# Gated mix of linear attention and a ReGLU layer: block products for down in seven first-half pairs, and one written order in the last projections

## The chip, the cores and the metric

The kernel runs on one core of one Trainium2 chip. The metric is the device time of one execution in microseconds (us). Before the change it is 1589.73 us, the median of three runs (1588.61 to 1591.07).

The core has five engines, each with its own queue of instructions that run in order: PE (TensorE, matrix products), DVE (VectorE), ACT (ScalarE), POOL (GpSimd) and SP (SyncE, which here only issues transfers). They wait for each other through semaphores.

## The reference

```python
def _A_ref(x, wqkv, w_phi, wo):          # linear attention, 32 heads of 18
    q, k, v = ...                         # x @ wqkv
    phi_q, phi_k = ...                    # softmax(+-(q or k) @ w_phi), joined
    kv, z = phi_k^T @ v, sum of phi_k
    return (phi_q @ kv) / (phi_q @ z + 1e-6) @ wo

def _B_ref(x, W_gate, W_up, W_down):
    gate = x @ W_gate
    up = x @ W_up
    gate = gate * (gate > 0)
    return (gate * up) @ W_down

g = _sigmoid((x * gate_w).sum(-1, keepdims=True))
return g * _A_ref(x, ...) + (1 - g) * _B_ref(x, ...)
```

All is float32, x has 2048 rows of 576, W_gate and W_up are 576 x 4608, W_down is 4608 x 576.

## The kernel before

Every float32 operand is split into a high part (rounded, made by ACT) and a low part (the rest, made by DVE), and a product is high x high + high x low + low x high on PE. Three stages follow each other.

**Attention (0 to about 340 us).** Keys, queries and values of 16 blocks of 128 rows, then for each of four blocks of 512 rows the sums, their inversion, `divide` (a matmul that spreads the inverse over the rows, a multiplication on DVE, then high part on ACT and low part on DVE) and `project_out`, which multiplies by the output weights and stores the rows to `att` in DRAM. `project_out(2, m)` and `project_out(3, m)` are the last ten. Between them the operands of the gated part are prepared: the weights of chunks 0 and 1 (`blocks`, `sums_of_blocks`, `block_sums`), and the seven operands of x (`operand_ahead` for three, `in_place` for four). PE, SP and POOL run that stage in program order (`in_order`). ACT and DVE are ordered by a scheduler there, with `behind` and `after` as limits.

**Gated part.** 4608 hidden columns are 36 chunks of 128, and a chunk for one half of the rows (1024) is a unit: units 0 to 35 for the first half, 36 to 71 for the second. Gate and up of a unit are formed together by seven products (a Strassen-Winograd scheme, `product`), one in each of seven steps j = 0 to 6, in the order 1, 5, 6, 2, 7, 3, 4. Each is 7 matmuls of 128x512. Products 1, 6, 7 and 4 gather in the PSUM tile `cx`, 5 and 3 in `ca`, 2 in `cy`. Partial sums are read from there on the way: g1 is a copy of `cx` after product 1 to which `cy` is added in step 4, u2 a copy of `ca` to which `cx` is added in step 5, g2 a copy of `cx` to which `ca` is added in step 6. Product 4 (step 6) may change `cx` only once u2 has read it.

Two chunks are a pair g. Its hidden tiles are ready after units 2g and 2g + 1, and the product with W_down (down) of pair q = g - 1 runs in the steps of units 2g (even) and 2g + 1 (odd), behind the product of each step. The addition of its result to the accumulators `ac` (DVE) follows one step later. In the second half pairs go by seven block products again (`down`: 14 products of 3 matmuls in two rows of blocks m = 0 and 1, and four of 2 matmuls for the last 64 columns). In the first half all pairs go plainly (`down_plain`: 8 outputs of 6 matmuls, two of 4). Block products need sums of down blocks (`down_sums_of_blocks`, POOL), differences of hidden tiles (`minus`, DVE), seven hidden tiles in high and low part in place of four, and 14 additions in place of 8. `plain_down` or `prepare_down` splits the raw down weights, `load_down` fetches the next.

In the first half the weights of the next chunk are also prepared in every unit: high parts on ACT, low parts `low_w` and, on 32 rows, `low_w_rows` on DVE, four sums of blocks on DVE. From unit 4 on a unit may end with one piece of `second_half`, which scales x for the second half (DVE). All five queues of the gated part are in program order, the order in which `step(u, j)` is written.

**End.** The last pair goes plainly, and the results are stored.

Of the kernel before, what the change touches and what calls it, by code (L numbers as in the profile page):

```python
# [15 lines left out]
P = 128  # L16
# [67 lines left out]
def gated_mix_kernel(  # L84
# [533 lines left out]
    def divide(b, k):  # L618

        R = RW[b]  # L620
# [4 lines left out]
        oh, ol = OW[b]  # L625
# [4 lines left out]
        nc.tensor.matmul(ps, spread[:, k], RD[b % 2], start=True, stop=True)  # L630
        r = R[:n, k]
        tt(out=r, in0=ps[:n], in1=r, op=MULT)
        nc.scalar.activation(oh[:n, k], r, AF.Copy)
        tt(out=ol[:, k] if k < 4 else oh[64:, k], in0=r, in1=oh[:n, k].bitcast(F32), op=SUB)
# [234 lines left out]
    def low_w_rows(o, a):  # L869
        tt(out=o[64:96, :, 2], in0=a[64:96, :, 2], in1=o[64:96, :, 2].bitcast(F32), op=SUB)  # L870
# [43 lines left out]
    def first_weights():  # L914
        with behind():
            blocks(0, high_w)
            low_parts(blocks, 0)
            sums_of_blocks(0)
        yield
        with behind():  # L920
            blocks(1, high_w)
            low_parts(blocks, 1)
        yield
        with behind():
            block_sums(0, high_w)
            sums_of_blocks(1)
        with behind():
            block_sums(1, high_w)
            low_parts(block_sums, 0)
        yield  # L930
        in_place(3)
        with behind():
            low_parts(block_sums, 1)
        yield
        for i in range(4, 7):
            in_place(i)
            yield

# [20 lines left out]
    def in_place(i):  # L959
        with behind():  # L960
            high_in_place(0, i)
            low_in_place(0, i)
            low_rest(0, i, tt)

    with in_order(tc, nc, nc.tensor, nc.sync, nc.gpsimd):
# [25 lines left out]
        for m in range(5):  # L991
# [11 lines left out]
            if m == 2:  # L1003
                with after(tc, nc, nc.vector, last_of(nc, nc.vector)):
                    invert(3)
                gather(3, 3, 2, 1, 0)
                whole(split_inverse(3))
                whole(x0)
        for m in range(5):
            project_out(2, m)  # L1010
            if m == 0:
                divide(3, 4)
                divide(3, 3)
                whole(x1)
            if m == 1:
                weights = first_weights()
                for k in (2, 1, 0):
                    divide(3, k)
                RS.close()
                pad = ctx.enter_context(tc.tile_pool(name="pad2", bufs=1, **R_))  # L1020
                pad.tile([P, 24], F32, name="pad2")
                xo2 = ctx.enter_context(tc.tile_pool(name="xo2", bufs=4, **R_))
                wop = ctx.enter_context(tc.tile_pool(name="wop", bufs=2, **R_))
                wraw = ctx.enter_context(tc.tile_pool(name="wraw", bufs=2, **R_))
                load_w(0)
                load_in_place(0, 3)
                load_rests(0, (3, 4, 5))
                load_w(1)
                for i in range(4, 7):
                    load_in_place(0, i)  # L1030
                whole(x2)
                load_rests(0, (6,))
                load_down(0)
                next(weights)
            if m > 1:
                next(weights)
        load_w(2)
        for m in range(5):
            project_out(3, m)
            if m < 3:  # L1040
                next(weights)
# [54 lines left out]
    def rest_weights(g, step):  # L1096
# [4 lines left out]
        elif step == 1:  # L1101
            tt(out=W4[g][:, 0:2, 1], in0=a, in1=W4[g][:, 0:2, 0].bitcast(F32), op=SUB)
            pt(out=a[:, 0], in0=a[:, 0], in1=a[:, 1], op=ADD)
# [38 lines left out]

    PLAIN = {1: (0, 0, 1), 2: (0, 1, 1), 3: (2, 0, 1), 4: (0, 0, 0), 5: (0, 1, 0), 6: (2, 0, 0),
# [35 lines left out]

    def down(g, s, bank):  # L1180
# [14 lines left out]
        if m == 0 and n in (1, 5, 2, 4):  # L1195
            w, r = {1: (0, 0), 5: (2, 1), 2: (1, 0), 4: (3, 1)}[n]
            if first and n in (1, 5):
                REST[r] = pm.tile([P, TB], F32, name=f"pm{r}")
            w = W4[g][:, w].rearrange("p s q -> p (s q)")
            mm(REST[r], w, h, first and n in (1, 5), False)  # L1200
            mm(REST[r], w, l, False, last and n in (2, 4))

        def add():
            i, t = ADDS[n]
            a = ACC[1, i, m, t]
# [116 lines left out]
    def step(u, j):  # L1322
# [4 lines left out]
        plain, was_plain = g < NG or g == 2 * NG - 1, q < NG  # L1327
# [3 lines left out]
        make = 0 < u < NC - 1  # L1331
        cx, ca, cy = (BANKS.get(n) for n in ("cx", "ca", "cy"))
# [20 lines left out]
        elif odd:  # L1353
            if j == 1:
# [28 lines left out]
        if make:  # L1383
# [4 lines left out]
            elif j == 1:  # L1388
                blocks(v, low_w)
                blocks(v, low_w_rows)  # L1390
# [4 lines left out]
            elif j == 4:  # L1395
                block_sums(v, low_w)
                block_sums(v, low_w_rows)
# [38 lines left out]
        if old and j == 5:  # L1436
            load_down(g)
# [30 lines left out]
        if j == 6 and u < NC:  # L1468
            if u >= 4:
# [163 lines left out]
```

## Time and profile before

| | |
|---|---|
| median of three runs | 1589.73 us |
| profiled execution | 1589.56 us |
| its span, first to last instruction | 1587.8 us |
| mean granted PE clock | 0.997 |
| POOL additions and subtractions on raw down weights (L1080 to L1083) | 136, all in the second half |

The page lists for each engine the time in which it was busy and its share of the span. The table of stretches gives the same for pieces of the span. A timeline row gives start, duration, engine, line, operation, output and inputs, the count of merged instructions, and in brackets the idle time before it with what ended it. Matmuls overlap: each lasts 0.39 us, but the next starts long before it ends, so the cost of one is read from starts or counts. A wait is the idle time that another engine or a transfer ended.

### The profile page before, as it was taken

The numbers are of one execution on the slowest core, as the hardware profiler recorded it, in microseconds if no ns is written. First come the engines' busy times: TensorE is split into PE (matmuls) and PEld (weight loads), VectorE is DVE, ScalarE is ACT, GpSimd is POOL, SyncE is SP. The second block draws the span as 40 slices with busy tenths as digits, with TensorE's granted clock in tenths as the row PEclk, the third lists the DMA queues.
The fourth block names the chain that finished last, engine by engine and source line by source line (L and its number), as shares of the span: only waits on it lengthen the run. The fifth ranks groups of instructions, "written<-read, shape, count | busy, mean of one in ns | idle before, by whom it ended". The sixth has DMA issues, their size and how long they took to land.

```text
span 1587.8 us, 20181 instructions
## 1 busy us (share of the span) xinstructions
PE 1570.8 (99%) x7823; PEld 1313.4 (83%) x7823; DVE 1190.8 (75%) x1865; ACT 559.0 (35%) x918; POOL 175.2 (11%) x243
## 2 busy tenths in 40 slices
PE   9999999999999999999999999999999999999998
PEld 9999995677888888888888888888888888888887
DVE  4997774577778777787777777777777777777777
ACT  4344335554333333333333334232233232222321
POOL 0126521110000000000000002111111111111110
PEclk9999999999999999999999999999999999999999
DMA  5365315587655576555554516543343343443432
GB/s 171 108 207 192 143 55 157 170 332 261 217 219 211 209 262 223 215 191 221 193 196 183 210 71 233 189 177 143 143 180 143 146 175 131 167 168 131 180 140 75
DMA packets 64539, 283.38 MB, mean 178 GB/s; under 512 B 6802, under 2 KB 17298, under 8 KB 55740
## 3 DMA queue, kind: packets, MB, share of 16 engines
q1 hardware_dynamic: 61228, 270.34, 47.0%
q0 software_dynamic: 2352, 10.11, 2.0%
q10 hardware_dynamic: 864, 1.65, 0.3%
q8 instruction: 61, 1.00, 0.3%
q14 instruction: 34, 0.28, 0.0%
HBM read 172.07 MB, written 108.60 MB: 177 GB/s over the span
## 4 chain that ended last, share of the span: by engine, by line
PE 95%; DVE 3%; ACT 1%; DMA 0%; issue 0%; POOL 0%; SPq 0%; ACTq 0%; POOLq 0%
PE cx L1128 29%; PE ca L1128 14%; PE pd L1168 12%; PE pd L1191 10%; PE cy L1128 7%; PE kv L175 4%; PE pk L175 3%; PE pq L175 3%; PE pm L1168 2%; PE pm L1191 2%; PE kv L421 1%; PE po L562 1%; PE pv L237 1%; PE pw L175 1%; PE ptr L379 1%; PE psf L259 1%
## 5 line engine op out<-in xcount | busy, mean ns | idle before, releaser
L1233 ACT ACTIVATE hh<-g 128x512 fp32r<-128x512 f32 x195 | 120.0, 624 | 458.5 <-DVE g L1290 289.2
L1206 DVE TENSOR_TENSOR ac<-pd,ac 128x512 f32<-128x512 f32 x238 | 164.1, 689 | 144.0 <-PE pd L1191 143.9
L1128 PE MATMUL cx<-xo,ws 128*128 128x512 f32 x1008 | 253.5, 391 | 3.3 <-ACT g L1294 3.3
L1128 PE MATMUL ca<-xo,ws 128*128 128x512 f32 x1008 | 251.9, 389 | 0.0
L1128 PE MATMUL cx<-xo,wb 128*128 128x512 f32 x1008 | 249.0, 389 | 1.5 <-DVE u L1415 1.5
L1128 PEld LDWEIGHTS cx<-xo,ws 128*128 128x128 f32 x1008 | 190.2, 189 | 43.3 <-ACT g L1294 3.7
L1128 PEld LDWEIGHTS cx<-xo,wb 128*128 128x128 f32 x1008 | 188.2, 188 | 42.5 <-DVE u L1415 1.9
L1128 PEld LDWEIGHTS ca<-xo,ws 128*128 128x128 f32 x1008 | 189.2, 188 | 39.3
L1168 PE MATMUL pd<-hh,wd 128*128 128x512 f32 x576 | 200.7, 389 | 0.0
L1191 PE MATMUL pd<-hh,wd 128*128 128x512 f32 x476 | 185.2, 389 | 0.0
L1174 DVE TENSOR_TENSOR ac<-pd,ac 128x512 f32<-128x512 f32 x144 | 99.1, 688 | 105.8 <-PE pd L1168 103.3
L1238 DVE TENSOR_TENSOR hl<-g,hh 128x512 fp32r<-128x512 f32 x195 | 135.7, 696 | 1.9 <-ACT hh L1233 0.2
L1294 ACT ACTIVATE g<-cx 128x512 f32<-128x512 f32 x144 | 85.0, 590 | 130.8 <-PE cx L1128 130.7
L1128 PE MATMUL cy<-xo,wb 128*128 128x512 f32 x504 | 127.3, 392 | 0.0
L1168 PEld LDWEIGHTS pd<-hh,wd 128*128 128x128 f32 x576 | 108.1, 188 | 22.6
L1091 ACT ACTIVATE wd<-wdr 128x384 fp32r<-128x384 f32 (+1 forms) x106 | 62.3, 606 | 143.4 <-DMA wdr<-wd 143.4
L1128 PEld LDWEIGHTS cy<-xo,wb 128*128 128x128 f32 x504 | 95.6, 190 | 20.0
L1168 PE MATMUL pd<-hl,wd 128*128 128x512 f32 x288 | 112.0, 389 | 0.0
L1191 PEld LDWEIGHTS pd<-hh,wd 128*128 128x128 f32 x476 | 89.3, 188 | 18.6
L1191 PE MATMUL pd<-hl,wd 128*128 128x512 f32 x238 | 92.6, 389 | 0.0
L831 POOL TENSOR_TENSOR xo<-xr,xo 32x512 fp32r<-32x512 f32 x5 | 8.3, 1669 | 615.9 <-ACT xo L847 615.9
L864 ACT ACTIVATE ws<-wr 128x1536 fp32r<-128x1536 f32 x36 | 53.7, 1491 | 46.6 <-DVE wr L888 46.6
(256 smaller groups left out, 2574.1 us busy)
## 6 DMA issues: line engine op xcount, KB each, us to landing
wsd<-ws SPq DMA_DIRECT2D x34, 1280.0 KB
ws<-wsd SPq DMA_DIRECT2D x34, 1280.0 KB
wbd<-wb SPq DMA_DIRECT2D x34, 960.0 KB
wb<-wbd SPq DMA_DIRECT2D x34, 960.0 KB
wr<-wgu SPq DMA_DIRECT2D x36, 768.0 KB
wdr<-wd SPq DMA_DIRECT2D x36, 576.0 KB
eT<-et SPq DMA_DIRECT2D x10, 594.0 KB
xt<-xb SPq DMA_DIRECT2D x7, 768.0 KB
```

The costliest lines, as they stand in the source:

```text
L175: nc.tensor.matmul(ps, w, m, start=i == 0, stop=i == len(pairs) - 1)
L237: nc.tensor.matmul(pv[i][c], m, w_[:, k, cs], start=k == 0 and n == 0, stop=k == 4 and n == 1)
L864: nc.scalar.activation(o[:, :, 0:3], a, AF.Copy)
L1091: nc.scalar.activation(o[:, 0], a, AF.Copy)
L1128: nc.tensor.matmul(ps, w, v, start=first and m == 0, stop=m == len(pairs) - 1, skip_group_check=True)
L1168: nc.tensor.matmul(ps, w, v, start=k == 0 and (i < 2 or first), stop=k == len(mms) - 1 and (i < 2 or last), skip_group_check=True)
L1174: tt(out=a, in0=ps, in1=a, op=ADD)
L1191: mm = lambda ps, w, v, a, z: nc.tensor.matmul(ps, w, v, start=a, stop=z, skip_group_check=True)
L1206: tt(out=a, in0=ps, in1=a, op=ADD)
L1233: nc.scalar.activation(h, src, AF.Copy)
L1238: tt(out=l, in0=src, in1=h.bitcast(F32), op=SUB)
L1294: nc.scalar.activation(a, ps, AF.Copy)
```

## The change

Two things are changed together.

Seven first-half pairs, g = 3, 5, 7, 9, 11, 13 and 15, take down by block products (`BY_BLOCKS`). The other first-half pairs stay plain. Their last 64 columns keep the plain weights, with one further hidden tile, key 8 (`REST_OF`), and so need no sums of those weights. In the odd unit of such a pair and in both units of the next one, the two operations of `low_w_rows` are run by POOL. The unit after such a pair has no piece of `second_half`. The raw down weights of a block pair that follows a plain one are fetched at step 1, not 5.

In the attention stage `divide` is cut in two (`quotient`, `operand_rows`). From the last block's divisions of k = 2, 1 and 0 on, ACT and DVE are in program order too, and the preparation of weights and operands is written out between the last projections.

```diff
+    def quotient(b, k):
...
         nc.tensor.matmul(ps, spread[:, k], RD[b % 2], start=True, stop=True)
         r = R[:n, k]
         tt(out=r, in0=ps[:n], in1=r, op=MULT)
+
+    def operand_rows(b, k):
...
         nc.scalar.activation(oh[:n, k], r, AF.Copy)
         tt(out=ol[:, k] if k < 4 else oh[64:, k], in0=r, in1=oh[:n, k].bitcast(F32), op=SUB)
...
+    def low_w_rows_aside(o, a):
+        low_w_rows(o, a, pt)
...
+        project_out(2, 0)
+        divide(3, 4)
+        divide(3, 3)
+        whole(x0)
+    with in_order(tc, nc, nc.tensor, nc.vector, nc.scalar, nc.gpsimd, nc.sync):
+        project_out(2, 1)
+        for k in (2, 1, 0):
+            quotient(3, k)
+        for k in (2, 1, 0):
+            operand_rows(3, k)
+        whole(x1)
...
+        project_out(3, 0)
+        block_sums(0, high_w)
+        low_parts(blocks, 1)
+        operand_low(0, 2)
+        load_rests(0, (6,))
         load_w(2)
+        low_parts(block_sums, 0)
+        high_in_place(0, 3)
+        project_out(3, 1)
+        low_of_place(3)
+        sums_of_blocks(1)
+        high_in_place(0, 4)
+        project_out(3, 2)
+        block_sums(1, high_w)
+        low_of_place(4)
+        high_in_place(0, 5)
+        project_out(3, 3)
+        low_parts(block_sums, 1)
+        low_of_place(5)
+        in_place(6)
+        project_out(3, 4)
...
+    BY_BLOCKS = range(3, NG - 2, 2)
+
+    def is_plain(g):
+        return g < NG and g not in BY_BLOCKS or g == 2 * NG - 1
...
+    REST_OF = ({1: (0, 0, 1), 5: (0, 1, 8), 3: (1, 1, 3), 2: (1, 0, 2)},
+               {1: (0, 0, 1), 5: (2, 1, 5), 2: (1, 0, 2), 4: (3, 1, 4)})
...
-        plain, was_plain = g < NG or g == 2 * NG - 1, q < NG
+        plain, was_plain = is_plain(g), is_plain(q)
...
+        rows_ = low_w_rows_aside if g in BY_BLOCKS and odd or q in BY_BLOCKS else low_w_rows
...
+            if g < NG and j < 2:
+                (high_h, low_h)[j]((g, 8), e2)
...
-                blocks(v, low_w_rows)
+                blocks(v, rows_)
...
-                block_sums(v, low_w_rows)
+                block_sums(v, rows_)
...
-        if old and j == 5:
+        if old and j == (1 if was_plain and not plain else 5):
             load_down(g)
...
-            if u >= 4:
+            if u >= 4 and not (old and q in BY_BLOCKS):
                 next(later_half, None)
```

The order of DVE around the start of unit 8, the even unit in which down of pair 3 begins. `ac` are additions into the accumulators, `hl` low parts of hidden tiles, `wb` and `ws` low parts of weights, `wr` sums of blocks, `g` and `u` the partial sums. Before, from the last addition of unit 7 to step 1 of unit 8:

```order
L1174 TENSOR_TENSOR ac<-pd_4622,ac 128x512
L1418 TENSOR_TENSOR g_4589<-ca,g_4589 128x512
L1290 SCALAR_TENSOR_TENSOR g_4589<-g_4589,u_4568 128x512
L335 TENSOR_TENSOR xb<-xb,ac 128x768
L1290 SCALAR_TENSOR_TENSOR g_4545<-g_4545,cx 128x512
L1238 TENSOR_TENSOR hl<-g_4589,hh 128x512
L867 TENSOR_TENSOR wb<-wr,wb 128x3x256
L870 TENSOR_TENSOR wb<-wr,wb 32x3x128
```

The same stretch of DVE with the change:

```order
L1190 TENSOR_TENSOR ac<-pd_4633,ac 128x512
L1442 TENSOR_TENSOR g_4596<-ca,g_4596 128x512
L1311 SCALAR_TENSOR_TENSOR g_4596<-g_4596,u_4572 128x512
L1308 TENSOR_TENSOR g_4414<-g_4596,g_4414 128x512
L335 TENSOR_TENSOR xb<-xb,ac 128x768
L1311 SCALAR_TENSOR_TENSOR g_4548<-g_4548,cx 128x512
L1308 TENSOR_TENSOR g_4457<-g_4596,g_4457 128x512
L1227 TENSOR_TENSOR ac<-pd_4671,ac 128x512
L1259 TENSOR_TENSOR hl<-g_4414,hh 128x512
L877 TENSOR_TENSOR wb<-wr,wb 128x3x256
L1102 TENSOR_TENSOR wd<-wdr,wd 128x384
```

Two differences (L1308), one addition and one pass over down weights come in, and the operation on 32 rows of `wb` goes to POOL.

Further on in unit 8 DVE had, before, from step 2 to u2 in step 5 (the three sums L885 to L887 ahead of it left out):

```order
L888 TENSOR_TENSOR wr<-wr 128x384
L1174 TENSOR_TENSOR ac<-pd_4695,ac 128x512
L867 TENSOR_TENSOR ws<-wr,ws 128x4x256
L870 TENSOR_TENSOR ws<-wr,ws 32x4x128
L1413 TENSOR_TENSOR g_4670<-cy,g_4670 128x512
L1174 TENSOR_TENSOR ac<-pd_4729,ac 128x512
L1415 TENSOR_TENSOR u_4693<-cx,u_4693 128x512
```

With the change DVE has there:

```order
L901 TENSOR_TENSOR wr<-wr 128x384
L1227 TENSOR_TENSOR ac<-pd_4671,ac 128x512
L1308 TENSOR_TENSOR g_4414<-g_4548,g_4414 128x512
L1259 TENSOR_TENSOR hl<-g_4457,hh 128x512
L1227 TENSOR_TENSOR ac<-pd_4695,ac 128x512
L1259 TENSOR_TENSOR hl<-g_4548,hh 128x512
L877 TENSOR_TENSOR ws<-wr,ws 128x4x256
L1437 TENSOR_TENSOR g_4692<-cy,g_4692 128x512
L1227 TENSOR_TENSOR ac<-pd_4671,ac 128x512
L1259 TENSOR_TENSOR hl<-g_4414,hh 128x512
L1439 TENSOR_TENSOR u_4721<-cx,u_4721 128x512
```

Three low parts, one difference and one addition more stand ahead of u2 (L1415, now L1439), and the row operation of `ws` is gone to POOL, where one of `wb`, the four sums of down blocks and one of `ws` now follow each other in each such unit.

The order of ACT at the end of the attention stage. `xo` are the high parts of x operands that are made in place, two rows for each; `o` are rows of a projection; the `g` at the end is the first copy of `cx`. Before:

```order
L864 ACTIVATE ws<-wr 128x4x384
L786 ACTIVATE o<-kv_3612 128x512
L864 ACTIVATE ws<-wr 128x4x384
L846 ACTIVATE xo<-xo 128x1024
L847 ACTIVATE xo<-xr 128x512
L846 ACTIVATE xo<-xo 128x1024
...
L847 ACTIVATE xo<-xr 128x512
L786 ACTIVATE o<-kv_3634 128x512
L788 ACTIVATE o<-kv_3652 64x512
L1294 ACTIVATE g_3716<-cx 128x512
```

With the change ACT has:

```order
L856 ACTIVATE xo<-xo 128x1024
L857 ACTIVATE xo<-xr 128x512
L796 ACTIVATE o<-kv_3602 128x512
L874 ACTIVATE ws<-wr 128x4x384
L856 ACTIVATE xo<-xo 128x1024
L857 ACTIVATE xo<-xr 128x512
L796 ACTIVATE o<-kv_3626 128x512
L856 ACTIVATE xo<-xo 128x1024
L857 ACTIVATE xo<-xr 128x512
L798 ACTIVATE o<-kv_3652 64x512
L1315 ACTIVATE g_3716<-cx 128x512
```

Of the four pairs of `xo` that stood between the weights `ws` of chunk 1 and the first copy of `cx`, two now stand ahead of those weights.

More of the change, by code (lines that the diff above doesn't have):

```diff
@@ L632, in divide @@
         tt(out=r, in0=ps[:n], in1=r, op=MULT)
+    def operand_rows(b, k):
+        n = P if k < 4 else 64
+        oh, ol = OW[b]
+        r = RW[b][:n, k]
         nc.scalar.activation(oh[:n, k], r, AF.Copy)
@@ L912, in low_parts @@
         f(u, low_w_rows)
[L914 to L937, printed above, removed]
     BEHIND = {}
@@ L959, in in_place, with low_of_place @@
     def in_place(i):
[L960 to L963, printed above, removed]
+        high_in_place(0, i)
+        low_of_place(i)
+    def low_of_place(i):
+        low_in_place(0, i)
+        low_rest(0, i, tt)
     with in_order(tc, nc, nc.tensor, nc.sync, nc.gpsimd):
@@ L1007, in gated_mix_kernel @@
                 whole(split_inverse(3))
[L1008 to L1036, printed above, removed]
```

44 lines of the change are left out of this document (33 added, 11 removed).

## The prediction

> **What bounds the kernel now.** I read the page first: the busy times, then the chain of work that ended last.
>
> ```profile
> PE 1570.8 (99%) x7823; PEld 1313.4 (83%) x7823; DVE 1190.8 (75%) x1865; ACT 559.0 (35%) x918; POOL 175.2 (11%) x243
> ...
> PE 95%; DVE 3%; ACT 1%; DMA 0%; issue 0%; POOL 0%; SPq 0%; ACTq 0%; POOLq 0%
> ```
>
> PE (TensorE) is nearly always busy and carries 95% of the chain. A matmul removed is therefore worth its own time, as long as nothing else becomes late, and any new wait of PE is lost in full. The table of 50 us stretches gives the price of a matmul and the room of the other engines. Its columns are length, then busy time and instructions of PE, weight loads, DVE, ACT and POOL, then PE's granted clock, DMA share and GB/s.
>
> ```profile
> 600.00:650.00 50.00, 50.00 (x222) 41.39 (x222) 40.16 (x61) 16.88 (x24) 0.00 (x0) 1.00 0.50 193
> 1050.00:1100.00 50.00, 50.00 (x222) 41.25 (x221) 35.84 (x60) 14.30 (x30) 6.44 (x14) 1.00 0.41 156
> ```
>
> In the first half of the gated part (600 to 650) PE does 222 matmuls in 50 us, one per 0.225 us. DVE (VectorE) is busy 40.2 of 50 us there, POOL (GpSimd) not at all. In the second half (1050 to 1100), where down already goes by block products and no gate and up weights are prepared, DVE has 35.8 of 50 us. So the first half, which is to get more DVE work, has the least room for it.
>
> PE's waits, the same for all times (total, times, longest), name the only other place with something to win, the stage around 300 to 372 us:
>
> ```profile
> PE cx L1128 <- ACT g L1294: 3.3, 1, 3.3
> PE cx L1128 <- DVE u L1415: 1.5, 1, 1.5
> PE kv L630 <- DVE R L632: 1.2, 2, 0.9
> ```
>
> **The matmuls removed.** A pair of chunks with plain down takes 8 outputs of 6 matmuls and 2 of 4, so 56; by block products 14 of 3 and 4 of 2, so 50. Seven pairs save 42 matmuls, 42 x 0.225 = **9.45 us**, if PE stays fed.
>
> **The DVE work added.** Each block pair adds on DVE 4 low parts of hidden tiles, 4 differences, 6 additions into the accumulators and four smaller passes over down weights in place of one long one. Six operations on 32 rows go from DVE to POOL. What matters is where this stands, since DVE now runs every operation in a written order. The timeline of DVE in a plain unit of before shows the distance from start to start (columns start, duration, instruction, idle before it):
>
> ```profile
> 603.42 0.69 DVE L1174 TENSOR_TENSOR ac<-pd,ac 128x512 f32<-128x512 f32 x1 [1.51 <-PE pd L1168]
> 604.02 0.68 DVE L1238 TENSOR_TENSOR hl<-g,hh 128x512 fp32r<-128x512 f32 x1
> 604.62 0.55 DVE L885 TENSOR_TENSOR wr<-wr 128x384 f32<-128x384 f32 x1
> 605.21 0.56 DVE L886 TENSOR_TENSOR wr<-wr 128x384 f32<-128x384 f32 x1
> ...
> 606.40 0.56 DVE L888 TENSOR_TENSOR wr<-wr 128x384 f32<-128x384 f32 x1
> 606.87 0.68 DVE L1174 TENSOR_TENSOR ac<-pd,ac 128x512 f32<-128x512 f32 x1
> 607.47 1.42 DVE L1094 TENSOR_TENSOR wd<-wdr,wd 128x1024 fp32r<-128x1024 f32 x2
> 608.81 1.22 DVE L867 TENSOR_TENSOR ws<-wr,ws 128x1024 fp32r<-128x1024 f32 x1
> ...
> 613.84 0.69 DVE L1174 TENSOR_TENSOR ac<-pd,ac 128x512 f32<-128x512 f32 x1 [1.20 <-PE pd L1168]
> 614.45 0.68 DVE L1418 TENSOR_TENSOR g<-ca,g 128x512 f32<-128x512 f32 x1
> 615.16 0.69 DVE L1290 SCALAR_TENSOR_TENSOR g<-g,u 128x512 f32<-128x512 f32 x1
> 615.77 0.95 DVE L335 TENSOR_TENSOR xb<-xb,ac 128x768 f32<-128x768 f32 x1
> 616.64 0.68 DVE L1290 SCALAR_TENSOR_TENSOR g<-g,cx 128x512 f32<-128x512 f32 x1
> ```
>
> An operation of 128x512 costs 0.60 us of DVE, 0.71 if the next one needs its result; four sums of blocks cost 3 x 0.59 + 0.47 = 2.24; an operation of 0.95 costs 0.87, and by the same 0.085 us of overlap one of 1.22 costs 1.14 and one of 0.55 costs 0.47.
>
> I count the worst unit, the even one after a block pair (unit 8, as the order of DVE in the part on the change shows it). Time 0 is where PE starts the unit. DVE was last idle for the addition in the step before: before, that stood 613.84 against a unit start of 613.64 + 7 x 0.225 = 615.21 by the row of PE,
>
> ```profile
> 613.64 3.34 PE L1128 MATMUL cx<-xo,wb 128*128 128x512 f32 x14
> ```
>
> so DVE starts at -1.37. From there to u2 = cx + ca stand: the step before, 0.60 + 0.71 + 0.71 + 0.60 (addition, g2, gate, difference); step 0, 0.87 + 0.60 + 0.60; step 1, 0.60 + 0.60 + 0.87 + 0.47; step 2, 0.60 + 0.60 + 2.24; step 3, 3 x 0.60; step 4, 0.60 + 0.60 + 1.14 + 0.60; step 5, 0.60 + 0.60 + 0.69. Together 17.30, so u2 is done at 15.93. PE wants it for product 4 after 42 product matmuls and 26 of down, 68 x 0.225 = 15.30. PE is stopped 0.63, and about 0.04 for the signal (before, 613.84 came that long after the matmul): **0.67 us**, with POOL costing nothing.
>
> In the odd unit after it (9) DVE catches up at step 2, 20 matmuls in (4.50, plus 0.20 until the last has drained and signalled: 4.70). Until u2 stand four additions, g1 and one low part (6 x 0.60), the sums (2.24), the low parts of the plain down weights (1.34, as 607.47 to 608.81) and of the sums' weights (1.14), and u2 itself (0.69): 9.01, done at 13.71. PE wants u2 after 60 matmuls, 13.50. Stop with the signal: **0.25 us**. The plain units in between are as before, where DVE waits for PE 1.51 and 1.20 us a unit by the rows above.
>
> **POOL beside DVE.** The first half of before has no POOL work, so the price of the six moved operations and of eight sums of down blocks per pair is read where POOL last ran beside DVE. First DVE, then POOL:
>
> ```profile
> 967.20 2.33 DVE L851 TENSOR_TENSOR xo<-xo 128x1024 fp32r<-128x1024 f32 x1
> 969.45 0.68 DVE L1174 TENSOR_TENSOR ac<-pd,ac 128x512 f32<-128x512 f32 x1
> 970.05 1.47 DVE L1238 TENSOR_TENSOR hl<-g,hh 128x512 fp32r<-128x512 f32 x1
> ```
>
> ```profile
> 967.16 1.28 POOL L831 TENSOR_TENSOR xo<-xr,xo 32x512 fp32r<-32x512 f32 x1 [3.90 <-ACT xo L847]
> 969.68 1.29 POOL L831 TENSOR_TENSOR xo<-xr,xo 32x512 fp32r<-32x512 f32 x1 [1.25 <-ACT xo L847]
> 971.58 4.46 POOL L831 TENSOR_TENSOR xo<-xr,xo 32x512 fp32r<-32x512 f32 x2 [0.61 <-ACT xo L847]
> 1004.07 0.46 POOL L1081 TENSOR_TENSOR wdr<-wdr 128x128 f32<-128x128 f32 x1
> ```
>
> A DVE operation of 128x1024 takes 1.22 us alone (608.81) and here 2.33, POOL having begun 0.04 us ahead of it; hl takes 0.68 alone (604.02) and 1.47. The addition that reads PSUM (969.45) is not touched, and POOL in turn is stretched (4.46 for two). So the two take turns where both read two SBUF operands, and a blocked DVE operation ends about 0.14 us earlier than POOL's end plus its own time (968.44 + 1.22 - 0.14 = 969.52; the row ends at 969.53). The Trainium skill, "SBUF — State Buffer", section "Who interferes with whom", says that a DVE instruction with two SBUF inputs and a GpSimd instruction that reads SBUF exclude each other, the later one blocked in full; these rows agree. It speaks against the change: by it alone, every meeting paid in full, the sum below would end at its upper bound, 1614.5.
>
> In unit 8 POOL has a row operation of 32x384, four of 0.46, and one of 32x512: about 0.96 to 1.28, 1.84 and 1.28, some 4.1 us, in a stretch in which DVE is never idle and most of its operations read two SBUF operands. Lost on DVE: nothing at the least, 4.1 - 6 x 0.14 = 3.3 at the most. On average an operation meets POOL half way, 2.05 - 0.84 = 1.2; as the long row operations come just when DVE does the low parts of the same weights, I take 1.5. Stop in unit 8: 2.2 us (0.67 to 4.0). In unit 9 the row operation of 1.28 becomes ready while DVE is between the low parts of wd and ws: 1.1 (0 to 1.14), a stop of 1.35 (0.25 to 1.4). Each stop also costs the first weight load:
>
> ```profile
> 307.64 0.50 PE L630 MATMUL kv<-rd,spread 128*128 128x512 f32 x1 [0.86 <-DVE R L632]
> 307.98 0.85 PE L175 MATMUL pw<-oh,wo 128*128 128x512 f32 x3
> ```
>
> 0.34 to the next matmul, not 0.225: 0.115. Per pair 2.2 + 1.35 + 0.23 = 3.78; seven pairs **+26.5 us** (8.1 to 39.4).
>
> **Other edits of that part.** ACT gets four high parts a pair and has 33 of 50 us free: nothing, within those 33 us. The hidden tiles turn through 8 buffers; the plain pair after a block pair takes the buffer that down's first product of the second block row just read. ACT waits there, with the copy of cx behind it, for which PE waits at product 6; but 10 matmuls (2.25 us) lie between, and ACT needs two operations of about 0.6 (as 346.37 below). The raw down weights land 3.4 us after their issue in the second half (1014.18 to 1017.55):
>
> ```profile
> 1014.18 0.33 SPq L908 DMA_DIRECT2D wdr<-wd  x1
> ```
>
> ```profile
> 1017.55 0.53 ACT L1091 ACTIVATE wd<-wdr 128x384 fp32r<-128x384 f32 x1 [7.94 <-DMA wdr<-wd]
> ```
>
> Issued at about 18 in unit 8 they are there 1.6 into unit 9, where ACT takes them at about 4.5: 2.9 us of cover, and what is later than that stops ACT and then PE.
>
> **The stage at 300 to 372 us, now in program order.** The longest wait, and the clock after it:
>
> ```profile
> 347.02 3.35 PE L1128 MATMUL cx<-xo,ws 128*128 128x512 f32 x7 [3.28 <-ACT g L1294]
> ```
>
> ```profile
> 346.00:347.00 1.00, 0.00 (x0) 0.67 1.04 438
> 353.00:354.00 1.00, 1.00 (x5) 0.92 1.07 450
> ```
>
> The wait began at 343.74. The clock's column, 0.67 in the slice from 346, says that it fell to half at about 346.3, 2.6 us into the wait; 0.92 in the slice from 353 says that it came back at 353.1. From 347.0 on that is 6.1 us at half speed, 3.0 us lost beside the 3.28. The 1.5 us wait for u was followed by no such fall. ACT held PE up:
>
> ```profile
> 337.89 1.49 ACT L864 ACTIVATE ws<-wr 128x1536 fp32r<-128x1536 f32 x1 [1.85 <-DVE wr L888]
> 339.29 1.04 ACT L846 ACTIVATE xo<-xo 128x1024 fp32r<-128x1024 f32 x1
> 345.16 0.57 ACT L786 ACTIVATE o<-kv 128x512 f32<-128x512 f32 x1
> 346.37 0.60 ACT L1294 ACTIVATE g<-cx 128x512 f32<-128x512 f32 x1
> ```
>
> Four operands (5.87 us) stand between the weights and the copy of cx. In the new order two of them stand ahead of those weights: 2.9 us less. But DVE's sums, which these weights wait for, now come behind one operand's low parts, up to 1.9 later. I take the wait as 1.7: a gain of 1.6, and of the 3.0 of the clock. Of the waits for the last divisions (1.2 in the last row of PE's waits) quotients first spare one round, 0.5; the 1.5 for u stays. Together **-5.0 us**, between +3 (a new wait of the old size) and -9.
>
> **The sum.** The profiled execution took 1589.56 (span 1587.8), the median of the runs is 1589.73: the same within 0.2. 1589.6 - 9.45 + 26.5 - 5.0 = 1601.65, say **1601.5 us**.
>
> **Rivals.**
> - Faster. POOL's operations fall beside those of DVE that read PSUM, or into waits, and block nothing. Then a pair stops PE 0.67 + 0.25 + 0.23 = 1.15, less than the 1.35 it saves: 1589.6 - 9.45 + 8.05 - 5.0 = 1583.2. It decides where a pair loses less than 1.35 + 5.0/7 = 2.06 us in all. For it: nothing in the first half of before shows POOL beside DVE. Against: 967 to 972. I give 0.20, the even milder case of no stops (1575) included.
> - Slower, by the clock. If the stop in unit 8 passes 2.6 us, half speed follows as at 346 us, 3.0 more per pair: 1601.5 + 21 = 1622.5. For it: 2.2 is near; against: the wait of 1.5 did nothing. 0.08. The Trainium skill, "TensorE: Matmul & The Clock Gate", Part 1, puts the fall after an idle window of about 3.4 us; here 2.6 were enough, so this rival is the nearer by the trace.
> - Even, so that the change does nothing in the end. Half the loss to POOL (1.3 instead of 2.6 per pair) gives 1601.5 - 9.1 = 1592.4, and with the stage at its better bound of -9, 1588.4: 0.12, of it 0.10 within the bound of no change.
>
> The forecast gets the remaining 0.60, with 1594 to 1617 from its own bounds. A difference of 0.2% (3.2 us) is about what a measurement of this kernel can tell from none. Below 1586.4: 0.20; within: 0.10; above: 0.70. The range takes in the first rival at its price and the forecast to its upper bound: 1583 to 1617.
>
> **What would show it.** Right: PE waits for DVE's u (the addition of u2) 14 times between 430 and 950 us, about 2 us in the even and 1.3 us in the odd units, with DVE busy over 46 of 50 us; low parts and sums of DVE there much longer than their 0.69, 1.22 and 0.56, each beside a POOL operation; first-half pairs of 50 down matmuls without a fall of the clock; one wait of 1 to 2 us at the first copy of cx. Wrong: unstretched DVE operations beside POOL; PE waiting for ACT's wd or a DMA; the clock falling in unit 8; no stops at all.

## The result and the profile after

| | before | after |
|---|---|---|
| median of four runs | 1589.55 us | 1598.03 us |
| range of the runs | 1588.61 to 1591.07 | 1597.15 to 1599.15 |
| profiled execution (span) | 1589.56 (1587.8) | 1599.15 (1597.4) |
| mean granted PE clock of it | 0.997 | 1.000 |

After over before is 1.0055, with a 95% interval of 1.004 to 1.007: the change makes the kernel about 8.7 us slower (8.5 between the medians). The prediction was 1601.5 us.

The page of after, busy times of the engines and the chain of work that ended last:

```profile
PE 1564.2 (98%) x7781; PEld 1304.4 (82%) x7781; DVE 1258.6 (79%) x1942; ACT 581.3 (36%) x967; POOL 259.9 (16%) x341
...
PE 83%; DVE 13%; issue 2%; ACT 1%; DMA 1%; POOL 0%; SPq 0%; DVEq 0%; ACTq 0%; POOLq 0%
```

PE has 42 matmuls fewer (7823 to 7781). DVE's share of the chain went from 3% to 13%: where PE did not wait between 430 and 950 us before, DVE now sets the end. The same stretch of the first half that was shown of before, in the table of stretches:

```profile
600.00:650.00 50.00, 47.40 (x209) 38.61 (x207) 47.70 (x69) 19.85 (x30) 12.20 (x14) 1.00 0.57 213
```

DVE is busy 47.7 of 50 us (40.2 before), POOL 12.2 (nothing before), and PE, which was never idle there, does 209 matmuls in place of 222. PE's waits of after (total, times, longest) name who stops it:

```profile
PE cx L1139 <- DVE u L1439: 20.6, 15, 1.7
PE cx L1139 <- ACT g L1315: 1.6, 1, 1.6
```

One of the 15 is the wait of 1.5 us at 363 us that before has too; the other 14 are two per block pair. The timeline of PE shows an even stop of the larger kind, with what stands around it, one of the smaller kind, and an odd stop (start, duration, instruction, idle time before it):

```profile
558.36 0.39 PE L1210 MATMUL pm<-hl,wd 128*128 128x512 f32 x1
560.47 1.89 PE L1139 MATMUL cx<-xo,wb 128*128 128x512 f32 x7 [1.71 <-DVE u L1439]
562.19 0.39 PE L1210 MATMUL pd<-hh,wd 128*128 128x512 f32 x1
...
630.28 0.39 PE L1210 MATMUL pm<-hl,wd 128*128 128x512 f32 x1
632.13 1.89 PE L1139 MATMUL cx<-xo,wb 128*128 128x512 f32 x7 [1.47 <-DVE u L1439]
```

```profile
504.32 0.39 PE L1210 MATMUL pd<-hh,wd 128*128 128x512 f32 x1
505.84 1.88 PE L1139 MATMUL cx<-xo,wb 128*128 128x512 f32 x7 [1.13 <-DVE u L1439]
```

The bracket is not yet the loss. A matmul lasts 0.39 us but costs 0.225, so the loss is start to start less 0.225: 560.47 - 558.36 - 0.225 = 1.88 us (four of the seven even units), 632.13 - 630.28 - 0.225 = 1.63 (the other three), 505.84 - 504.32 - 0.225 = 1.30 (all odd units). The seven matmuls after a stop take 562.19 - 560.47 = 1.72 in place of 1.575, so 0.15 more is lost at each. Together 4 x 1.88 + 3 x 1.63 + 7 x 1.30 + 14 x 0.15 = 23.6 us.

What made DVE late in unit 8 is read from DVE and POOL side by side. DVE:

```profile
475.16 0.91 DVE L1259 TENSOR_TENSOR hl<-g,hh 128x512 fp32r<-128x512 f32 x1
...
478.53 0.81 DVE L898 TENSOR_TENSOR wr<-wr 128x384 f32<-128x384 f32 x1
479.38 0.70 DVE L899 TENSOR_TENSOR wr<-wr 128x384 f32<-128x384 f32 x1
480.11 0.70 DVE L900 TENSOR_TENSOR wr<-wr 128x384 f32<-128x384 f32 x1
...
481.32 0.68 DVE L1227 TENSOR_TENSOR ac<-pd,ac 128x512 f32<-128x512 f32 x1
...
483.73 1.23 DVE L1259 TENSOR_TENSOR hl<-g,hh 128x512 fp32r<-128x512 f32 x1
```

POOL in the same unit:

```profile
474.38 1.14 POOL L880 TENSOR_TENSOR wb<-wr,wb 32x384 fp32r<-32x384 f32 x1 [8.66 <-ACT wb L874]
477.55 0.46 POOL L1088 TENSOR_TENSOR wdr<-wdr 128x128 f32<-128x128 f32 x1 [2.03 <-DVE wd L1102]
478.08 0.84 POOL L1089 TENSOR_TENSOR wdr<-wdr 128x128 f32<-128x128 f32 x1
479.00 0.66 POOL L1090 TENSOR_TENSOR wdr<-wdr 128x128 f32<-128x128 f32 x1
...
483.11 1.29 POOL L880 TENSOR_TENSOR ws<-wr,ws 32x512 fp32r<-32x512 f32 x1 [2.72 <-issue]
```

The first hl stands beside the row operation of wb and takes 0.91 in place of 0.68 (+0.23). The four sums of blocks run from 478.53 to 481.32, 2.79 in place of 2.24 (+0.55), while POOL does its sums of down blocks. The last hl shown stands beside the row operation of ws (+0.55). The addition into `ac` right ahead of it, from 483.13 us, has one operand in PSUM, runs beside the same row operation and is not stretched (0.69 us). That is 1.33 us in this unit.

In unit 9 one single meeting, an operation of DVE that has to wait for one of POOL, costs nearly everything. Groups of after between 430 and 950 us (count, busy time, mean ns): the low part of the last 64 columns of the down weights, 128x128, seven times in the odd units after block pairs, takes 1.38 us; the same work of a plain pair, without a meeting, in the odd unit two units earlier (L1110), 0.28:

```profile
L1102 DVE TENSOR_TENSOR wd<-wdr,wd 128x128 fp32r<-128x128 f32 x7 | 9.7, 1384 | 0.0
...
L1110 DVE TENSOR_TENSOR wd<-wdr,wd 128x128 fp32r<-128x128 f32 x7 | 1.9, 279 | 0.0
```

### The profile page after: what moved, and what is told of

Read it like the earlier page. It is cut to its first block, busy times and chain, and to the rows that moved or that the text cites. A ratio compares the mean times of both kernels' runs of the same rounds, so it can differ in the third digit from the quotient of the medians.

```text
span 1597.4 us, 20440 instructions
## 1 busy us (share of the span) xinstructions
PE 1564.2 (98%) x7781; PEld 1304.4 (82%) x7781; DVE 1258.6 (79%) x1942; ACT 581.3 (36%) x967; POOL 259.9 (16%) x341
## 4 chain that ended last, share of the span: by engine, by line
PE 83%; DVE 13%; issue 2%; ACT 1%; DMA 1%; POOL 0%; SPq 0%; DVEq 0%; ACTq 0%; POOLq 0%
PE cx L1139 25%; PE ca L1139 12%; PE pd L1210 11%; PE pd L1184 7%; PE cy L1139 6%; PE kv L175 4%; PE pk L175 3%; PE pq L175 3%; DVE ac L1227 2%; DVE hl L1259 2%; PE pm L1210 2%; PE pm L1184 1%; DVE ws L877 1%; PE kv L421 1%; PE pv L237 1%
## 5 line engine op out<-in xcount | busy, mean ns | idle before, releaser
L1227 DVE TENSOR_TENSOR ac<-pd,ac 128x512 f32<-128x512 f32 x336 | 230.8, 687 | 154.5 <-PE pd L1210 152.8
L1254 ACT ACTIVATE hh<-g 128x512 fp32r<-128x512 f32 x223 | 137.0, 625 | 451.6 <-DVE g L1311 226.7
L1139 PEld LDWEIGHTS ca<-xo,ws 128*128 128x128 f32 x1008 | 189.2, 188 | 39.4
L1259 DVE TENSOR_TENSOR hl<-g,hh 128x512 fp32r<-128x512 f32 x223 | 158.8, 712 | 0.7 <-ACT hh L1254 0.2
L1210 PEld LDWEIGHTS pd<-hh,wd 128*128 128x128 f32 x672 | 126.1, 188 | 26.2
L1210 PE MATMUL pd<-hl,wd 128*128 128x512 f32 x336 | 130.8, 389 | 0.0
L1099 ACT ACTIVATE wd<-wdr 128x384 fp32r<-128x384 f32 (+1 forms) x120 | 69.2, 587 | 134.1 <-DMA wdr<-wd 134.1
L1190 DVE TENSOR_TENSOR ac<-pd,ac 128x512 f32<-128x512 f32 x88 | 60.5, 688 | 54.2 <-PE pd L1184 51.6
L880 POOL TENSOR_TENSOR wb<-wr,wb 32x384 fp32r<-32x384 f32 x21 | 24.7, 1174 | 383.7 <-ACT wb L874 250.2
L1102 DVE TENSOR_TENSOR wd<-wdr,wd 128x384 fp32r<-128x384 f32 (+1 forms) x120 | 84.5, 712 | 0.0
L1184 PEld LDWEIGHTS pd<-hh,wd 128*128 128x128 f32 x352 | 66.1, 188 | 13.8
L1210 PEld LDWEIGHTS pd<-hl,wd 128*128 128x128 f32 x336 | 63.1, 188 | 13.2
```

Source lines behind the costliest of these rows:

```text
L880: f(out=o[64:96, :, 2], in0=a[64:96, :, 2], in1=o[64:96, :, 2].bitcast(F32), op=SUB)
L1099: nc.scalar.activation(o[:, 0], a, AF.Copy)
L1102: tt(out=o[:, 1], in0=a, in1=o[:, 0].bitcast(F32), op=SUB)
L1139: nc.tensor.matmul(ps, w, v, start=first and m == 0, stop=m == len(pairs) - 1, skip_group_check=True)
L1184: nc.tensor.matmul(ps, w, v, start=k == 0 and (i < 2 or first), stop=k == len(mms) - 1 and (i < 2 or last), skip_group_check=True)
L1190: tt(out=a, in0=ps, in1=a, op=ADD)
```

## The experiments

Diffs are against the changed kernel. Times are medians, each ratio is to the kernel before in runs on the same chip, with its 95% interval.

**1. The stage alone.** No first-half pair goes by block products.

```diff
-    BY_BLOCKS = range(3, NG - 2, 2)
+    BY_BLOCKS = range(0)
```

> The new order of the last projections alone; all first-half pairs stay plain. Theory A (the block pairs cost, the stage gains): the first copy of cx waits 1.6 us for ACT and the clock does not fall, the first u waits 1.5; no wait for u between 430 and 950 us; about 1585 us, 4 to 5 below the kernel before. Theory C (the stage is what costs): above 1590 us.

Measured 1583.57 us, ratio 0.9966 (0.9952 to 0.9979), so about -5.4 us, without any wait for u between 430 and 950 us. The stage pays for itself. One of the five runs took 4071.25 us, for which nothing on record gives a reason; the ratio leaves it out, and the other four lie between 1583.21 and 1583.70.

**2. The block products alone**, with the old order of the stage.

```diff
-    with in_order(tc, nc, nc.tensor, nc.vector, nc.scalar, nc.gpsimd, nc.sync):
-        project_out(2, 1)
-        for k in (2, 1, 0):
-            quotient(3, k)
...
+                weights = first_weights()
+                for k in (2, 1, 0):
+                    divide(3, k)
...
+        for m in range(5):
+            project_out(3, m)
+            if m < 3:
+                next(weights)
```

> The block pairs alone, with the last projections ordered as before. Theory A: the wait of 3.3 us and the clock at half after it as before, then 14 waits for u of 1.5 to 1.7 and 1.1 us; 42 matmuls less (-9.45) and 14 stops (+23): about 1603 us. Theory C: below 1590 us.

Measured 1603.39 us, ratio 1.0093 (1.0078 to 1.0109): about +14.8 us. The two halves add up: 14.8 - 5.4 = 9.4, and both together gave 8.7. The loss is all in the block pairs.

**3. POOL's part left out.** The sums of down blocks of the first-half pairs and the six 32-row operations per pair are not computed by anyone.

```diff
     def down_sums_of_blocks(g, m):
+        if g < NG:
+            return
...
-        rows_ = low_w_rows_aside if g in BY_BLOCKS and odd or q in BY_BLOCKS else low_w_rows
+        rows_ = (lambda o, a: None) if g in BY_BLOCKS and odd or q in BY_BLOCKS else low_w_rows
```

> As changed, but with POOL's operations of the first half left out: the six operations on 32 rows and the eight sums of raw down blocks of each block pair are not computed. DVE keeps its order and its count. Theory A (POOL and DVE exclude each other): the stops shrink to what DVE's own length makes, shown idle of about 0.5 in the even and 0.1 in the odd unit in place of 1.5 to 1.7 and 1.1; low parts and sums on DVE back at 0.69 and 0.56; 1598 - 7 x (1.2 + 1.05) = about 1582 us. Theory B (the length of DVE's order alone makes the stops, POOL costs nothing): unchanged, 1598 us.

Measured 1579.20 us, ratio 0.9939 (0.9925 to 0.9952), 18.8 us below the changed kernel. PE's waits for u are then

```profile
PE cx L1141 <- DVE u L1441: 3.2, 5, 1.5
```

so 1.5 as ever and four of about 0.42, in the even units. In the odd units no idle time is left, though product 4 still starts 0.19 us late by start to start (501.71 - 501.29 - 0.225 in unit 9). The work that is left out is POOL's alone, DVE's list is unchanged, and yet DVE is what becomes faster: POOL's operations cost PE 18.8 of the 23.6 us. The rest fits what is still lost, 4 x 0.58 + 7 x 0.19 + 11 x 0.15 = 5.3 us.

**4. The 32-row operations back on DVE.**

```diff
-        rows_ = low_w_rows_aside if g in BY_BLOCKS and odd or q in BY_BLOCKS else low_w_rows
+        rows_ = low_w_rows
```

> As changed, but the operations on 32 rows stay on DVE in all units; POOL keeps the sums of down blocks. By DVE's rows they cost 0.55 + 0.68 and the overlap with their neighbours, about 1.5 us a unit. Theory A1 (moving them to POOL still frees DVE of more than the meetings cost): even stops grow by about 0.9, odd ones by 0 to 0.3: 1603 us (1600 to 1606). Theory A2 (the moved rows cost all they relieve, and more): stops shrink, 1590 to 1596 us.

Measured 1607.59 us, ratio 1.0114 (1.0101 to 1.0128). The bracket in front of product 4 is 2.08 or 1.60 in the even units and 1.33 in the odd ones, about 0.4 or 0.1 and 0.2 more than in the changed kernel. POOL is the cheaper place for them, but by little: most of what DVE is spared comes back as waiting (experiment 10, without these operations, shows 0.85 or 0.40 and no idle time in the odd units). In two of the seven even units of this profile, an execution of 1604.98 us, the clock fell as well, which is taken up under 8 and makes 3.4 us of the difference. The other three runs took 1607.16 to 1608.40 at a lower mean clock (0.996 or 0.997, against 0.998); that it fell more often in them is likely, but no profile shows it.

**5. u2 first.** The addition of u2 goes to the start of step 5, ahead of the addition into `ac` and the low part of a hidden tile.

```diff
         product(ps, u, SEQ[j], first)
+        if j == 5:
+            tt(out=T["u2"], in0=BANKS["cx"], in1=T["u2"], op=ADD)
         add_up()
...
-        elif j == 5:
-            tt(out=T["u2"], in0=cx, in1=T["u2"], op=ADD)
```

> As changed, but DVE makes u2 at the start of step 5, ahead of an addition and, in the even unit, a low part: 1.2 us earlier there, 0.6 in the odd unit. No work is added or taken away. Theory A (PE waits for the place of u2 in DVE's order): even stops shrink by about 1.0, odd ones by 0 to 0.6, unless u2 only meets POOL's operations another way: 1585 to 1592 us. Theory D (DVE is simply full, its place does not matter): the waits move to the additions and the time stays within 2 us of 1598.

Measured 1589.82 us, ratio 0.9998 (0.9989 to 1.0007). The even stop shows about 0.54 in place of 1.7 (0.28 in place of 1.47 in three units), but the odd one 1.16, as before, though u2 has one addition less ahead of it. In DVE's timeline of this run

```profile
491.52 1.76 DVE L877 TENSOR_TENSOR wb<-wr,wb 128x768 fp32r<-128x768 f32 x1
```

wb's low part, 0.95 in the changed kernel's unit 9, now meets POOL's row operation of the same weights (490.93 to 492.47). The even stop is shorter, so DVE is earlier in unit 9 and runs into a meeting that it had missed: +0.8 for -0.6.

**6. u2 first, `ws` behind it.** The low parts of `ws` go behind u2 too, and the row operations of the odd unit after a block pair go back to DVE.

```diff
-        rows_ = low_w_rows_aside if g in BY_BLOCKS and odd or q in BY_BLOCKS else low_w_rows
+        rows_ = low_w_rows_aside if g in BY_BLOCKS and odd or q in BY_BLOCKS and not odd else low_w_rows
...
-            elif j == 4:
+            elif j == 5:
                 block_sums(v, low_w)
                 block_sums(v, rows_)
-            elif j == 5:
                 if v < NC - 2:
```

> As e5, and the low parts of the sums' weights, which are needed a unit later, are made after u2 in step 5 in place of step 4, in all first-half units; and in the odd unit after a block pair the operations on 32 rows stay on DVE. Theory A: u2 comes 2.3 us earlier than in the change in the even unit, which is more than its stop of 1.9, so that it goes; 0.3 to 0.8 is left in the odd unit and after: 1577 to 1581 us, below both kernels. Theory D: 1595 or more.

Measured 1577.13 us, ratio 0.9925 (0.9913 to 0.9938): 12 us below before, 21 below the changed kernel, with nothing left out. No wait for u is left in the gated part (four of about 0.2 us for ACT's copy of `cx` come in, and one of 0.8 for an addition at 375 us in place of the wait for u at 363), and between 600 and 650 us PE is never idle although DVE is busier than in the changed kernel:

```profile
600.00:650.00 50.00, 50.00 (x220) 40.81 (x219) 48.38 (x74) 19.57 (x30) 6.64 (x7) 1.00 0.69 253
```

**7. The same order without block products** (experiment 6 with `BY_BLOCKS = range(0)`).

> The order of e6 with all first-half pairs plain. Theory A: in plain pairs nobody waits for u2, so the order is worth nothing by itself: 1585 us, as the stage alone, so that e6 is 5 to 8 us below it by its 42 matmuls. Rival: the order itself is what gains, and this is as fast as e6 or faster.

Measured 1584.18 us, ratio 0.9963 (0.9950 to 0.9975), the same as the stage alone. So the order of 6 gives nothing by itself; it lets the block products keep 7.05 of their 9.45 us. Experiment 6 differs from 5 in two things, the place of the `ws` low parts and the row operations of the odd unit; which of them does it was not run apart.

**8. No POOL at all in the first half:** rows as in 4, and the sums of down blocks on DVE.

```diff
-        pt(out=a[:, 2], in0=a[:, 2], in1=a[:, 3], op=ADD)
...
+        f = pt if g >= NG else tt
+        f(out=a[:, 2], in0=a[:, 2], in1=a[:, 3], op=ADD)
...
```

> As changed, but the operations on 32 rows and the sums of raw down blocks of the first half all run on DVE; POOL has nothing there. DVE gets about 1.5 us of rows and 1.25 of sums in a block unit, and meets nobody. Theory A: even stops of about 3.4 in one or two waits, odd 1.3 to 1.6: 1607 to 1612 us. Theory A2 (POOL beside DVE is the whole cost): 1582 to 1590 us.

Measured 1620.21 us, ratio 1.0191 (1.0175 to 1.0206), 8 us above the upper end of what was expected. The stops for u are no longer than the longest of 4, 2.05 to 2.09 in the seven even units and 1.33 in the odd ones, and four even units have a further wait for a low part of a hidden tile:

```profile
PE pd L1211 <- DVE hl L1260: 2.8, 4, 0.7
```

But after six of the seven even stops the matmuls run slower; unit 24 in PE's timeline:

```profile
786.91 0.39 PE L1211 MATMUL pm<-hl,wd 128*128 128x512 f32 x1
789.34 3.35 PE L1140 MATMUL cx<-xo,wb 128*128 128x512 f32 x7 [2.05 <-DVE u L1440]
```

and the same place in the table of stretches (the clock is the third column from the right):

```profile
788.00:789.00 1.00, 0.00 (x0) 0.00 (x0) 1.00 (x3) 0.00 (x0) 0.00 (x0) 1.00 1.18 492
789.00:790.00 1.00, 0.66 (x2) 0.56 (x3) 1.00 (x3) 0.00 (x0) 0.00 (x0) 0.64 0.84 348
790.00:791.00 1.00, 1.00 (x4) 0.81 (x3) 1.00 (x2) 0.00 (x0) 0.00 (x0) 0.50 0.92 330
791.00:792.00 1.00, 1.00 (x3) 0.78 (x3) 0.78 (x2) 0.09 (x1) 0.00 (x0) 0.50 0.74 166
792.00:793.00 1.00, 1.00 (x4) 0.79 (x3) 0.00 (x0) 0.76 (x2) 0.00 (x0) 0.65 1.03 379
```

The clock is at half from 789.28 (0.64 = 0.28 + 0.72 / 2) to 792.70. Six falls of 3.42 us at half speed are 10.3 us; with the 1607 to 1612 that were expected this makes 1617 to 1622, which takes in the measured time.

**9 and 10. POOL's two kinds of work left out one at a time:** in 9 the sums of down blocks, in 10 the 32-row operations (the first and the second of the two edits of 3).

> As the changed kernel, but POOL's sums of a pair's down part in the first half are not computed (nothing is put in their place); its 32-row operations stay. Theory A (POOL's loss is shared by short sums and long row operations, each holding VectorE up where it meets it): the stop in the second unit of a pair falls from 1.5-1.7 shown to 1.0-1.3, the one in the next unit stays at 1.13, so about 7 x 0.5 = 3.5 us less than the changed kernel, 1594 to 1595 us. Rival B (the 32-row operations alone make the whole loss): neither stop changes, 1598 us. Rival C (the sums make it): both go, about 1580 us.

> As the changed kernel, but the 32-row operations on ws and wb are not computed in the seven units that have products for a whole block and the seven units behind them; POOL's sums of the down part stay. Theory A: the stop in the next unit goes (at most 0.1 shown) and the one in the second unit falls to 0.5-1.0, so 7 x (1.2 + 0.6..1.0) = 12.6 to 15.4 us less than the changed kernel, 1582.6 to 1585.4 us. Rival B: everything goes that leaving all of POOL's first-half work out took, 1579 us. Rival C: neither stop changes, 1598 us.

9 measured 1589.15 us (0.9999, 0.9989 to 1.0008), 10 measured 1583.54 us (0.9961, 0.9946 to 0.9976). 10 came as expected for shared costs: 0.85 or 0.40 is left of the even stop and no idle time of the odd one. In 9 the even stop fell to about 1.15 or 0.9, about as expected, but 9 saved 8.9 us where 3.5 were expected, and the reason is in the odd unit, in which no sum runs. First DVE of 9, then POOL:

```profile
497.80 1.42 DVE L1104 TENSOR_TENSOR wd<-wdr,wd 128x1024 fp32r<-128x1024 f32 x2
499.13 0.68 DVE L1229 TENSOR_TENSOR ac<-pd,ac 128x512 f32<-128x512 f32 x1
499.73 1.71 DVE L877 TENSOR_TENSOR ws<-wr,ws 128x1024 fp32r<-128x1024 f32 x1
```

```profile
498.93 1.43 POOL L880 TENSOR_TENSOR ws<-wr,ws 32x512 fp32r<-32x512 f32 x1 [7.00 <-ACT ws L874]
```

The two low parts of wd, 128x1024 and 128x128, take their 1.42 us undisturbed: the short one had the turn, and POOL's operation was held up by it (1.43 in place of 1.29). POOL then ends at 500.36 and ws pays +0.49. In the changed kernel the same three rows are

```profile
499.74 2.52 DVE L1102 TENSOR_TENSOR wd<-wdr,wd 128x1024 fp32r<-128x1024 f32 x2
502.18 0.68 DVE L1227 TENSOR_TENSOR ac<-pd,ac 128x512 f32<-128x512 f32 x1
502.78 1.21 DVE L877 TENSOR_TENSOR ws<-wr,ws 128x1024 fp32r<-128x1024 f32 x1
```

with POOL's operation from 500.83 to 502.11: it had the turn ahead of the short low part, which could start only 0.04 us later (499.74 + 1.21 - 0.085 = 500.87), and that one paid 1.10. So the odd stop shows 0.53 us in 9 and 1.13 in the changed kernel, and what decides is less than a tenth of a microsecond. This also is why the two parts alone do not add up to the whole: 9 and 10 left 10.0 and 4.3 us above 3 (1579.20), together 14.3, while both together cost 18.8.

## Why the prediction was right

- **Matmuls removed, -9.45 us: held.** 42 fewer are counted, and experiment 6 keeps 7.05 us of the price once PE is fed.
- **Fourteen stops for u2, two per pair: held**, place by place, between 485 and 937 us, with DVE at 47.7 of 50 us and no wait for ACT's wd or a transfer.
- **Even stop without POOL, 0.67 us: about right for four units, not for three.** With the 0.165 by which loss exceeds the bracket, experiment 3 shows 0.42 + 0.165 = 0.58. The working took the worst unit for all seven. Units 16, 28 and 32 have no piece of `second_half` at step 0 (0.87 us on DVE) and would not stop at all, 0.58 - 0.87 = -0.29.
- **POOL's part of it, taken as 1.5 of 0 to 3.3: 1.33 in unit 8** by the rows above. In the units without the piece DVE comes 0.87 us earlier and the row operation of wb meets wb's low part in full, in unit 16

```profile
618.76 1.77 DVE L877 TENSOR_TENSOR wb<-wr,wb 128x768 fp32r<-128x768 f32 x1
```

  1.77 in place of 0.95. That makes 0.82 + 0.55 + 0.55 = 1.92 of POOL's loss there, and -0.29 + 1.92 = 1.63, as measured; in unit 8 it is 0.58 + 1.33 = 1.91 against 1.88. So the term was 2.2 a pair and came to 1.88 or 1.63: too high by 3.0 us over the seven. It is the term that was mis-sized most, and luck kept the miss small: in the three units without the piece DVE's own stop was far too large and POOL's part too small, which cancel in part. The Trainium skill, "SBUF — State Buffer", section "Who interferes with whom", gives the exclusion, and the meetings shown here agree with it; how much is paid follows from how much of the other operation is left when the two meet, not from an average.
- **Odd stop, 1.35 (0.25 + 1.1): 1.30.** DVE's own part was 0.19 (experiment 3), and POOL's is the 1.384 - 0.279 = 1.10 us of the short low part of wd. The place was named (the row operation of ws becomes ready between the low parts of wd and ws), but that the full price was paid is luck: by experiment 9 it hangs on less than a tenth of a microsecond, and at other timings the same operation costs 0.49.
- **Restart, 0.115 a stop: 0.15**, 0.5 us more over the 14.
- **The stage, -5.0: -5.4** (-7.6 to -3.3) by experiment 1. The wait for the first copy of `cx` was taken as 1.7:

```profile
345.49 1.89 PE L1139 MATMUL cx<-xo,ws 128*128 128x512 f32 x7 [1.64 <-ACT g L1315]
```

  The fall of the clock, credited with 3.0 us in full, does not come in every execution of the old order. Experiment 2 keeps that order, and its profile shows the old wait with full speed behind it (seven matmuls in 1.89 us, 3.35 before):

```profile
349.14 1.89 PE L1144 MATMUL cx<-xo,ws 128*128 128x512 f32 x7 [3.27 <-ACT g L1320]
```

  The -5.0 met the -5.4 in part by luck. From PE's first `gates` matmul (L320) to the start of this product the old order takes 58.05 us (58.07 in experiment 2), the new one 54.26 (54.31 in experiment 1). That is 3.8 less, where 1.6 and 0.5 were credited: the waits around the last divisions also went from 0.86, 0.43 and 0.61 to one of 0.40. The clock's part is 2.9 where the fall comes, and nothing where it does not.
- **The sum.** 23.6 in place of 26.5 and 5.4 in place of 5.0 take 3.3 us off 1601.5: 1598.2, against 1598.03 measured. The agreement is closer than the runs of the changed kernel allow, which spread over 2.0 us. The ends of the forecast's range, 1594 and 1617, do not come out of its terms: with the bounds that it gives, 8.1 to 39.4 and -9 to +3, these make 1579 to 1622.5.
- **Rival, POOL blocks nothing (1583.2):** its price was 4.0 us too high (experiment 3, 1579.2, without POOL's work, with 5.3 us of stops where 8.05 were taken), and its condition was not met.
- **Rival, even (1592.4):** it needed half the loss to POOL, 9.1 us; POOL's operations cost 18.8 (experiment 3).
- **Rival, the clock (1622.5):** it did not happen, but its threshold was wrong. The prediction read from one wait that 2.6 us of idling are needed. Experiments 4 and 8 have it after stops of 2.08, only 0.4 longer than those of the changed kernel. It was much nearer than its 0.08 said. A fall after a stop also costs 1.7 us there, not 3.0.

## What to carry to other kernels

Work moved from a full engine to an idle one is only moved if the two can run at once. Here POOL's 32-row operations held up DVE for most of the time that they took off it: the even stop of unit 8 shows 2.08 us with them on DVE (experiment 4), 1.69 with them on POOL, and 0.85 without them (experiment 10). The operations that were held up read two SBUF operands; an addition from PSUM beside them was not. When a kernel is fed by an engine at 95%, the order of the operations in front of what the next engine waits for is worth more than their number: an addition, a low part of a hidden tile and the low parts of `ws` put behind u2, and the row operations of one unit put back, turned about +9 us into -12. And measure such a change on every variant: a meeting of two operations costs 0 to 1.1 us according to shifts of less than 0.1 us, so gains of single parts do not add up.

## What the runs showed of the hardware

**The clock is judged on a fixed grid.** In experiment 8 the clock falls at 564.00, 639.10, 714.18, 789.28, 864.38 and 939.46 us (each worked out from the slice in which it changes, as at 789), and comes back 3.42 us later. The distances are 75.1 us, 22 x 3.413 (75.09). In experiment 4 the two falls, at 561.36 and 779.82, lie 64 x 3.413 apart. The first of them in the table of stretches:

```profile
561.00:562.00 1.00, 1.00 (x5) 0.73 (x4) 0.96 (x3) 0.00 (x0) 0.00 (x0) 0.68 0.95 233
...
564.00:565.00 1.00, 1.00 (x4) 0.77 (x4) 0.80 (x2) 0.22 (x1) 0.00 (x0) 0.61 1.01 412
```

With such a grid laid over each run, it is not the length of a wait that decides but its share within one window of 3.41 us. Experiment 4 has both outcomes for the same wait:

```profile
487.08 1.89 PE L1139 MATMUL cx<-xo,wb 128*128 128x512 f32 x7 [2.08 <-DVE u L1439]
...
706.47 1.89 PE L1139 MATMUL cx<-xo,wb 128*128 128x512 f32 x7 [2.09 <-DVE u L1439]
...
779.33 2.96 PE L1139 MATMUL cx<-xo,wb 128*128 128x512 f32 x7 [2.08 <-DVE u L1439]
```

| wait | most of it in one window | fall |
|---|---|---|
| 8, before 489.51 (2.09) | 1.49 | no |
| 4, before 487.08 (2.08) | 1.27 | no |
| 4, before 706.47 (2.09) | 1.75 | no |
| 2, before 349.14 (3.27) | 1.78 | no |
| 8, before 789.34 (2.05) | 1.99 | yes |
| 4, before 559.97 (2.08) | 2.02 | yes |
| 4, before 779.33 (2.08) | 2.08 | yes |
| the kernel before, before 347.02 (3.28) | 2.60 | yes |

The rows of experiment 2 and of the kernel before stand on grids of their own. The clock falls once more at the end of these runs, a few microseconds behind the last matmul, and this fall lies on the grid of the earlier ones: at 1618.72 in experiment 8 (0.86 in its slice), 243 x 3.413 behind the one at 789.28; at 1602.44 in experiment 4 (0.72), 241 x 3.413 behind 779.82; at 1585.38 in the kernel before (0.69), 363 x 3.413 behind 346.34. In experiment 2, which has no other fall, the clock reads 0.67 in the slice from 1600 us, so it falls at 1600.34. A line of its grid then lies 367 windows earlier, at 347.65, near the middle of the wait of 3.27 (345.87 to 349.14), and cuts it into 1.78 and 1.49.

So between 1.78 and 1.99 us of idling in a window of 3.41, a little over half, the clock falls for the next window. In experiment 8 the even stops follow each other about as fast as 22 windows (74.0 to 75.6 against 75.1 us), so most of them lie alike in the grid. The Trainium skill, "TensorE: Matmul & The Clock Gate", Part 1, states a free-running window of 3413 ns, and the distances agree; that less than a whole idle window is enough is what these runs add. In the old stage the wait began at 343.74 and the fall came at 346.34, 2.60 us into it, with 0.68 us of waiting left in the next window, after which the clock stayed low for one window more. That this share, well below 1.78, was enough to keep the clock low is not explained by the table and stays open. The longest stop of the changed kernel, 1.71, is below the 1.78 that passed without a fall wherever the grid lies.

**The first stage varies.** PE's first `gates` matmul (L320) started at 288.97 us in the profile of before, 291.23 in that of after, 291.07 in experiment 2 and 289.17 in experiment 1, ahead of everything that the change touches. So 2.3 us of the 9.6 between the two profiled executions come from ahead of the change. Single runs of one kernel spread by up to 4.6 us (15 runs of the kernel before, 1588.49 to 1593.09), and differences below that need the medians of several runs.
